# Decay attention and token/channel mixer on one core: weight casts behind the turned copies, low parts and conversions shifted, last sum with tokens on partitions

## The chip, the cores and the metric

The kernel runs on one core of a Trainium2 chip. The metric is device microseconds (us) from launch to end. The kernel before took 600.77 us (median of three runs, 600.35 to 603.7). The profiled execution is a separate one, with its own time.

TensorE is called PE here (PEld is its weight load), VectorE DVE, ScalarE ACT, GpSimd POOL, SyncE SP. SPq and ACTq are the DMA queues that SP and ACT issue into.

## The reference

The program is a chunked linear attention with a decay per head, followed by an MLP mixer. q, k, v are `[4, 8, 768, 64]` (batch, heads, tokens, head size).

```python
for b in range(nb):                      # blocks of 64 tokens
    intra = einsum('bhic,bhjc->bhij', qb, kb) * Dmask[None]
    intra = einsum('bhij,bhjd->bhid', intra, vb)
    inter = einsum('bhid,bhde->bhie', qb * lam_pow[None], kv_state)
    out[:, :, sl] = intra + inter
    kv_state = lam_block * kv_state + einsum('bhsd,bhse->bhde', kb * rev_pow, vb)
x  = out as [4, 768, 512]
u  = x + (relu(x^T @ w_tok1) @ w_tok2)^T          # w_tok1 768x256, w_tok2 256x768
y  = u + relu(u @ w_ch1) @ w_ch2                  # w_ch1 512x1536, w_ch2 1536x512
```

The mixer's weights arrive as 64-bit numbers. The kernel converts each to two 32-bit parts, a high and a low one (`w1h`, `w1l` and so on), and forms each product of the mixer as three matmuls: high by high, low by high, high by low.

## The kernel before, in words

Attention runs over 16 passes `i`, one for each pair of heads of a batch (`pairs`, four passes to a batch). It is a pipeline that is written out by hand: the order of the calls in the loop is the order of the instructions on every engine, and nothing reorders them. In pass `i` PE does `scores(i+1)` (tiles `sc`), the first half of `outputs(i)` (`xT`), the state products of pass `i+1` (`kv`), the second half of `outputs(i)`, the transposes of k and q for pass `i+2` (`kt`, and `qt` up to pass 4; from pass 5 on DVE turns q with `STREAM_TRANSPOSE`), and `turn_back(i)` (`xp`), which turns the attention output so that tokens lie on partitions. From pass 4 on, groups of matmuls of the token mixer (`ph`, `pu`) are put between these, by the table `take`.

ACT copies `xT` to `uT[b]`, copies `kt` and `qt` to `kT` and `qT`, and casts `xp` to the high part `xhi` (L354). DVE masks the scores (`a`, L299), scans the state (`sv`, L265), subtracts to get `xlo` (L355). POOL scales q (`qs`, L244), scales a part of k (`kd`, L239) and places the state (`stb`, L278, two copies). The PSUM tag `sh` has three banks, which `kv`, `kt`, `qt`, `xp`, `ph` and `pu` take in turn: a tile may start when the tile three before it has been read. So the first `xp` or `qt` behind two `kt` waits for the scan `sv` that reads `kv`. The tag `xT` has one bank.

A weight conversion (`narrow`) is eight entries of a queue `waiting`: ACT takes the magnitude (L379), DVE does five operations on 128x512 words (L380, L383, L386, L389, L392), one entry is empty, and `split` casts the high part on ACT (L374) and subtracts the low part on POOL (L375). `later(n)` takes `n` entries from that queue at fixed places in a pass. The three parts of `w_tok1` are queued in passes 0 to 2, those of `w_tok2` in passes 2 and 3 (two of them in pass 3), the four parts of the first quarter group of the channel weights in passes 6 to 9. Batches' `uT` tiles that are not yet written serve as room for raw words and results: `uT[3]` is written by attention from pass 12 on.

The channel mixer runs over six groups of hidden columns (`g`) and eight blocks of 384 tokens (`k`): `mm1` (L640), relu on ACT and low part on DVE, then `mm2` of the unit before (L661), whose result DVE adds to `uT` (L666). In all of it channels lie on partitions. In the last group the results of blocks 0 to 6 are turned by DVE and written in pieces of 32 channels; the last block is turned by PE in `finish`, copied, and written.

Of the kernel before, what the change touches and what calls it, by code (L numbers as in the profile page):

```python
# [21 lines left out]
def kernel(  # L22
# [23 lines left out]
    nc = tc.nc  # L46
# [16 lines left out]
    waiting = deque()  # L63

# [270 lines left out]
    def turn_back(i, g):  # L335
# [19 lines left out]
        nc.vector.tensor_sub(out=lo, in0=src, in1=hi.bitcast(F32))  # L355
# [7 lines left out]
    def narrow(raw, a, sg, hi, lo, view):  # L363
# [9 lines left out]
        def split():  # L373
            nc.scalar.copy(out=hi, in_=view(af))  # L374
            nc.gpsimd.tensor_sub(out=lo, in0=view(af), in1=hi.bitcast(F32))  # L375

        waiting.extend(
            [
                lambda: nc.scalar.activation(af, high.bitcast(F32), AF.Abs),  # L379
# [12 lines left out]
                lambda: nc.vector.scalar_tensor_tensor(  # L392
                    out=a, in0=a, scalar=0x7FFFFFFF, in1=sg, op0=ALU.bitwise_and, op1=ALU.bitwise_or
                ),
                lambda: None,
                split,
            ]
        )

# [84 lines left out]
    def load_group(g, pool, scratch):  # L484
# [19 lines left out]
        def convert(i):  # L504
            raw, a, sg = space[i]
            raw = raw.rearrange("p (n two) -> p n two", two=2)
            if i < 2:
                ts = slice(2 * i, 2 * i + 2)
                narrow(raw, a, sg, c1h[:, ts], c1l[:, ts], lambda x: x.rearrange("p (t f) -> p t f", t=2))
            else:  # L510
                narrow(raw, a, sg, c2h[:, i - 2], c2l[:, i - 2], lambda x: x)
# [43 lines left out]
    for i in range(-2, NI):  # L555
# [23 lines left out]
        if place:  # L579
            place()  # L580
        later(1 if work else 2)
        n = early.get(i, len(work) // 4)
        cuts = [0, n, max(n, (3 * len(work) + 1) // 4 if len(work) > 2 else len(work) // 2), len(work)]
        for n in range(3):
            for f in work[cuts[n] : cuts[n + 1]]:
                f()
                later(2 if len(work) < 3 else 1)
            if n < 2 and i >= 0:
                turn_back(i, n)
                later(1 if work else 2 + n)  # L590
            if n == 0 and i + 2 < NI:
                scale_k(i + 2)
        if 0 <= i + 3 < NI and i >= -1:
            load_v(i + 3)
# [8 lines left out]
        if 2 <= i < 4:  # L603
            convert_w2(i - 2)
        if i == 3:
            convert_w2(2)
        if i == 5:
# [5 lines left out]
        if i == 9:  # L613
            waiting.extend(split_block(0, up))
    later(99)
    att.close()
# [35 lines left out]
    def mm2(g, k, t, between=None):  # L652
# [5 lines left out]
        for jj in range(JG):  # L658
# [4 lines left out]
            if between and jj == 0:  # L663
                between()
        ub = uT[b][:, t, sh * SB : (sh + 1) * SB]
        nc.vector.tensor_add(out=ub, in0=po, in1=ub)  # L666
        if g < NG - 1 or k == len(blocks) - 1:
            return
# [12 lines left out]
    def finish(t, ylast):  # L681

        k = len(blocks) - 1
        b, sh = blocks[k]
        yp = bank("sh", f"yp{t}", SB)
        for c in range(SB // P):
            cs = slice(c * P, (c + 1) * P)
            nc.tensor.transpose(
                out=yp[:, cs], in_=uT[b][:, t, sh * SB + c * P : sh * SB + (c + 1) * P], identity=ident
            )  # L690
        es = slice(t * P, (t + 1) * P)
        src = yp.rearrange("p (c e) -> p c e", e=P)
        if t == 3:
            nc.vector.tensor_copy(out=ylast[:, :, es], in_=src)
        else:
            nc.scalar.copy(out=ylast[:, :, es], in_=src)
        to = out[b, sh * SB : (sh + 1) * SB].rearrange("(c s) e -> s c e", s=P)
        if t > 0:
            es = slice(0 if t == 1 else t * P, (t + 1) * P)
            (nc.sync if t == 2 else nc.scalar).dma_start(out=to[:, :, es], in_=ylast[:, :, es])  # L700
# [33 lines left out]
    ylast = cp.tile([P, SB // P, DM], F32, name="ylast")  # L734
    mm2(*units[-1], 0)
    mm2(*units[-1], 1)
    mm2(*units[-1], 2, between=lambda: finish(0, ylast))
    finish(1, ylast)
    mm2(*units[-1], 3, between=lambda: finish(2, ylast))
    finish(3, ylast)  # L740

# [26 lines left out]
```

## Time and profile before

| | |
|---|---|
| median of three runs | 600.77 us |
| the profiled execution, whole | 602.27 us |
| its span, first to last instruction | 600.5 us |
| PE busy | 581.5 us, 97% |
| DVE busy | 349.3 us, 58% |
| mean granted TensorE clock | 0.994 |

The span is cut by the profile into 40 slices of 15 us. PE is below nine tenths in the first five of them and in the last, and the clock row shows 9 instead of full in two of the same five. From about 72 us on PE is busy without a gap that matters until the last 5 us. The two stages that have room are the first 72 us and the tail.

### The profile page before, as it was taken

Reading aid. Unit: us, or ns where it says so; the run is one execution under the profiler, and the core shown is the slowest. Engines: PE = TensorE matmul, PEld = TensorE weight load, DVE = VectorE, ACT = ScalarE, POOL = GpSimd, SP = SyncE. Lnnn points to the kernel's source line nnn. Section 1 sums busy time; section 2 is a strip of 40 time slices with the busy share of each in tenths; the row PEclk is TensorE's granted clock in tenths of the full one; section 3 lists DMA queues with packets and bytes.
Section 4 is the critical chain, followed back from the end, with each engine's and each line's share of the span. In section 5 each row is a group of like instructions: output and inputs, shape, how many; then the busy total and the mean of one; then the engine's idle time right before and its main releaser. Section 6 shows DMA issues by size and latency. Waiting matters only on the chain.

```text
span 600.5 us, 10671 instructions
## 1 busy us (share of the span) xinstructions
PE 581.5 (97%) x4378; PEld 566.3 (94%) x4378; DVE 349.3 (58%) x663; ACT 155.4 (26%) x322; POOL 139.0 (23%) x131
## 2 busy tenths in 40 slices
PE   5979899999999999999999999999999999999997
PEld 5868799889999999999999999999999999999996
DVE  4588777886733667446534664446534664356654
ACT  3454423444223243212201221012211221011011
POOL 5646533364215358201100010001100010000000
PEclk9989899999999999999999999999999999999999
DMA  9999899999100112011200111011200200016667
GB/s 186 240 229 172 140 175 164 191 175 161 37 11 27 37 36 70 1 33 38 71 1 0 61 47 35 1 36 41 66 1 0 71 1 1 0 21 90 89 90 134
DMA packets 169648, 44.73 MB, mean 74 GB/s; under 512 B 162816, under 2 KB 163968, under 8 KB 169600
## 3 DMA queue, kind: packets, MB, share of 16 engines
q1 hardware_dynamic: 165456, 42.88, 37.6%
q10 hardware_dynamic: 4144, 1.18, 0.9%
q8 instruction: 34, 0.56, 0.4%
q14 instruction: 14, 0.11, 0.1%
HBM read 37.75 MB, written 6.29 MB: 73 GB/s over the span
## 4 chain that ended last, share of the span: by engine, by line
PE 87%; DVE 6%; DMA 4%; ACT 2%; issue 1%; SPq 0%; ACTq 0%; DVEq 0%
PE ph L640 34%; PE po L661 33%; PE ph L449 6%; PE pu L469 4%; PE xT L314 3%; PE sc L290 3%; PE xT L324 2%; DMA kn<-in_k_dram 2%; DMA uT<-in_moe_w_tok_dram 2%; PE xp L346 1%; DVE xlo L355 1%; PE kv L257 1%; DVE uT L383 1%; DVE a L299 1%; DVE uT L389 1%
## 5 line engine op out<-in xcount | busy, mean ns | idle before, releaser
L645 DVE SCALAR_TENSOR_TENSOR hl<-ph,hh 128x384 fp32r<-128x384 f32 x96 | 53.5, 558 | 164.9 <-ACT hh L644 164.9
L661 PE MATMUL po<-hh,c2h 128*128 128x384 f32 x384 | 129.4, 337 | 0.0
L640 PE MATMUL ph<-uh,c1h 128*128 128x384 f32 x384 | 129.2, 337 | 0.0
L640 PE MATMUL ph<-ul,c1h 128*128 128x384 f32 x384 | 129.2, 336 | 0.0
L640 PE MATMUL ph<-uh,c1l 128*128 128x384 f32 x384 | 129.1, 336 | 0.0
L661 PE MATMUL po<-hh,c2l 128*128 128x384 f32 x384 | 128.8, 335 | 0.0
L661 PE MATMUL po<-hl,c2h 128*128 128x384 f32 x384 | 128.6, 335 | 0.0
L644 ACT ACTIVATE hh<-ph 128x384 fp32r<-128x384 f32 x96 | 47.3, 492 | 299.5 <-PE ph L640 297.8
L666 DVE TENSOR_TENSOR uT<-po,uT 128x384 f32<-128x384 f32 x192 | 104.7, 552 | 23.5 <-PE po L661 23.4
L661 PEld LDWEIGHTS po<-hh,c2l 128*128 128x128 f32 x384 | 72.1, 188 | 0.0
L640 PEld LDWEIGHTS ph<-ul,c1h 128*128 128x128 f32 x384 | 72.1, 188 | 0.0
L661 PEld LDWEIGHTS po<-hl,c2h 128*128 128x128 f32 x384 | 72.1, 188 | 0.0
L640 PEld LDWEIGHTS ph<-uh,c1h 128*128 128x128 f32 x384 | 72.1, 188 | 0.0
L661 PEld LDWEIGHTS po<-hh,c2h 128*128 128x128 f32 x384 | 72.0, 188 | 0.0
L640 PEld LDWEIGHTS ph<-uh,c1l 128*128 128x128 f32 x384 | 72.0, 188 | 0.0
L375 POOL TENSOR_TENSOR c1l<-wa,c1h 128x512 fp32r<-128x512 f32 x10 | 12.9, 1292 | 179.9 <-ACT c1h L374 179.9
L534 POOL TENSOR_TENSOR ul<-uT,uh 128x384 fp32r<-128x384 f32 x32 | 36.0, 1157 | 37.4 <-ACT uh L533 37.4
L314 PE MATMUL xT<-a,vn 128*64 128x128 f32 x384 | 37.1, 285 | 4.3 <-ACT uT L331 4.3
L278 POOL COPY stb<-sv 64x320 f32<-64x320 f32 x32 | 26.7, 834 | 43.6 <-DVE sv L265 42.7
L299 DVE TENSOR_TENSOR a<-sc,mask 128x384 f32<-128x384 f32 x64 | 31.2, 549 | 5.8 <-PE sc L290 5.7
L324 PE MATMUL xT<-qs,stb 128*64 128x128 f32 x320 | 32.0, 278 | 0.0
L314 PEld LDWEIGHTS xT<-a,vn 128*64 128x64 f32 x384 | 22.8, 139 | 8.3 <-ACT uT L331 4.7
(80 smaller groups left out, 756.9 us busy)
## 6 DMA issues: line engine op xcount, KB each, us to landing
raw<-in_moe_w_ch_dram SPq DMA_DIRECT2D x20, 512.0 KB, 3.6
vn<-in_v_dram SPq DMA_DIRECT2D x16, 384.0 KB, 5.4
kn<-in_k_dram SPq DMA_DIRECT2D x30, 192.0 KB, 5.3
out_dram<-y SPq DMA_DIRECT2D x108, 48.0 KB, 1.9
qn<-in_q_dram SPq DMA_DIRECT2D x44, 96.0 KB, 4.1
uT<-in_moe_w_tok_dram SPq DMA_DIRECT2D x2, 1536.0 KB, 8.5
kr<-in_k_dram SPq DMA_DIRECT2D x32, 96.0 KB, 4.1
uT<-in_moe_w_ch_dram SPq DMA_DIRECT2D x4, 512.0 KB, 5.3
```

The lines of the kernel that those rows point to most:

```text
L278: nc.gpsimd.tensor_copy(out=st[r, :, h, :], in_=sv[r].rearrange("p (e c) -> p c e", c=NC - 1))
L299: nc.vector.tensor_mul(out=a, in0=sc[h].rearrange("p (c i) -> p c i", i=P), in1=mask[:, 2 * p + h, None, :].broadcast_to([P, 3, P]),)
L314: nc.tensor.matmul(out=xT[h * D : (h + 1) * D, cs], lhsT=vns[i][:, h, c, :], rhs=weights_of[i, g, h][:, cg, :], start=(cg == 0), stop=False,)
L324: nc.tensor.matmul(out=xT[h * D : (h + 1) * D, cs], lhsT=st[:, c - 1, h, :], rhs=qss[i][:, c - 1, :], start=False, stop=(cg == 2),)
L449: nc.tensor.matmul(out=ph, lhsT=w[:, c, fs], rhs=x[:, c], start=(i == 0), stop=(i == 3 * NC - 1))
L469: nc.tensor.matmul(out=pu, lhsT=h[:, kk, cs], rhs=w[:, kk, ss], start=(i == 0), stop=(i == 3 * NK - 1))
L534: nc.gpsimd.tensor_sub(out=ul[:, t], in0=ub[:, t], in1=uh[:, t].bitcast(F32))
L640: nc.tensor.matmul(out=ph, lhsT=w[:, ct, js], rhs=x[:, ct], start=(i == 0), stop=(i == 11))
L644: nc.scalar.activation(hh, ph, AF.Relu)
L645: nc.vector.scalar_tensor_tensor(out=hl, in0=ph, scalar=0.0, in1=hh.bitcast(F32), op0=ALU.max, op1=ALU.subtract)
L661: nc.tensor.matmul(out=po, lhsT=w[:, jj, cs], rhs=h, start=(i == 0), stop=(i == 3 * JG - 1))
L666: nc.vector.tensor_add(out=ub, in0=po, in1=ub)
```

## The change

Four things. (1) `split` (cast on ACT and low part on POOL) leaves the queue `waiting` and goes to a list `casts`, which is emptied at set places: behind the copies of turned k and q in each pass, in front of the next conversion's magnitude, and at the end of pass 5. A held conversion is then six entries of `waiting` instead of eight. (2) `turn_back` no longer subtracts `xlo` itself: it returns the subtraction, which runs at once in passes with token work and after the next `later` in passes without. (3) The three parts of `w_tok2` are queued in passes 2, 3, 4 instead of 2, 3, 3, and the loads and conversions of the first channel group one pass later. (4) The last block's `mm2` is done with tokens on partitions: the hidden tile is the stationary operand, 128 tokens by 512 channels are one sum (`pe`), for the last 128 tokens two sums of 256. What is added, `u`, is turned by PE beforehand, in the last group behind blocks 2, 4 and 6 (`turn_last`), copied to `ylast` by ACT, and the sum goes to memory from there without another turn.

```diff
-        nc.vector.tensor_sub(out=lo, in0=src, in1=hi.bitcast(F32))
+        return lambda: nc.vector.tensor_sub(out=lo, in0=src, in1=hi.bitcast(F32))
...
+        def magnitude():
+            flush()
+            nc.scalar.activation(af, high.bitcast(F32), AF.Abs)
+        def join():
+            nc.vector.scalar_tensor_tensor(
+                out=a, in0=a, scalar=0x7FFFFFFF, in1=sg, op0=ALU.bitwise_and, op1=ALU.bitwise_or
+            )
+            casts.append(split)
...
-                lambda: None,
-                split,
+                join,
...
         if place:
             place()
+        flush()
         later(1 if work else 2)
...
-                turn_back(i, n)
+                split_low = turn_back(i, n)
+                if work:
+                    split_low()
                 later(1 if work else 2 + n)
+                if not work:
+                    split_low()
...
-        if 2 <= i < 4:
+        if 2 <= i < 5:
             convert_w2(i - 2)
-        if i == 3:
-            convert_w2(2)
-        if 5 <= i < 9:
-            load(i - 5)
         if 6 <= i < 10:
-            convert(i - 6)
+            load(i - 6)
+        if 7 <= i < 11:
+            convert(i - 7)
...
+    def finish(c, y):
+        n = 2 if c == SB // P - 1 else 1
+        for e in range(n):
+            es = slice(e * DM // n, (e + 1) * DM // n)
+            po = bank("sc", f"pe{c}{e}", DM // n)
...
+                    nc.tensor.matmul(out=po, lhsT=h[:, cs], rhs=w[:, jj, es], start=(i == 0), stop=(i == 3 * JG - 1))
...
+            nc.vector.tensor_add(out=y[:, c, es], in0=po, in1=y[:, c, es])
+            (nc.sync if n == 2 and e == 0 else nc.scalar).dma_start(out=to, in_=y[:, c, es])
+    def turn_last(c, y):
+        yp = bank("sh", f"yp{c}", DM)
...
+        nc.scalar.copy(out=y[:, c], in_=yp)
...
+            if x == 0 and g == NG - 1 and k in (2, 4, 6):
+                turn_last(k // 2 - 1, ylast)
+    for c in range(SB // P):
+        finish(c, ylast)
```

On ACT, around pass 2, the cast of the first third of `w_tok1` moves. Before (`xT20` and `xT21` are the two halves of pass 2's output, `kt4`, `qt4` the turned k and q for pass 4):

```order
L354 CAST xhi00_332<-xp11_462 128x3x128
L374 CAST w1h_129<-uT1_61 128x512
L331 COPY uT0_60<-xT20_508 128x384
L331 COPY uT0_60<-xT21_533 128x384
L213 COPY kT4_548<-kt40_549 128x384
L213 COPY kT4_548<-kt41_554 128x384
L229 COPY qT4_547<-qt40_559 128x384
L229 COPY qT4_547<-qt41_564 128x384
L379 ACTIVATE uT1_61<-uT3_63 128x512
```

The same stretch of ACT in the changed kernel, whose lines are numbered anew (L380 is the cast, L385 the magnitude):

```order
L360 CAST xhi00_332<-xp11_462 128x3x128
L337 COPY uT0_60<-xT20_506 128x384
L337 COPY uT0_60<-xT21_531 128x384
L219 COPY kT4_546<-kt40_547 128x384
L219 COPY kT4_546<-kt41_552 128x384
L235 COPY qT4_545<-qt40_557 128x384
L235 COPY qT4_545<-qt41_562 128x384
L380 CAST w1h_129<-uT1_61 128x512
L385 ACTIVATE uT1_61<-uT3_63 128x512
```

The cast has gone from in front of six copies to behind them, and now stands just ahead of the next part's magnitude. The same holds for the second third, around pass 3; the last third's cast still stands ahead of the copy of `xT40`.

On DVE, in pass 3, from the turn of q for pass 5 to the first masked scores. Before:

```order
L218 STREAM_TRANSPOSE qT5_671<-qn5_474 128x768
L380 TENSOR_SCALAR uT1_61<-uT3_63 128x512
L383 SCALAR_TENSOR_TENSOR uT1_61<-uT3_63,uT1_61 128x512
L355 TENSOR_TENSOR xlo01_575<-xp30_689,xhi01_574 128x3x128
L386 TENSOR_SCALAR uT1_61<-uT1_61 128x512
L389 TENSOR_SCALAR uT1_61<-uT1_61 128x512
L392 SCALAR_TENSOR_TENSOR uT1_61<-uT1_61 128x512
L355 TENSOR_TENSOR xlo01_575<-xp31_701,xhi01_574 128x3x128
L380 TENSOR_SCALAR uT3_63<-uT2_62 128x512
L299 TENSOR_TENSOR a500_729<-sc500_721,mask_80 128x384
```

And in the changed kernel (L396 to L405 and L388 are the five conversion operations in their order, L361 is `xlo`):

```order
L224 STREAM_TRANSPOSE qT5_669<-qn5_472 128x768
L396 TENSOR_SCALAR uT1_61<-uT3_63 128x512
L399 SCALAR_TENSOR_TENSOR uT1_61<-uT3_63,uT1_61 128x512
L402 TENSOR_SCALAR uT1_61<-uT1_61 128x512
L405 TENSOR_SCALAR uT1_61<-uT1_61 128x512
L388 SCALAR_TENSOR_TENSOR uT1_61<-uT1_61 128x512
L361 TENSOR_TENSOR xlo01_575<-xp30_689,xhi01_574 128x3x128
L396 TENSOR_SCALAR uT3_63<-uT2_62 128x512
L399 SCALAR_TENSOR_TENSOR uT3_63<-uT2_62,uT3_63 128x512
L402 TENSOR_SCALAR uT3_63<-uT3_63 128x512
L361 TENSOR_TENSOR xlo01_575<-xp31_701,xhi01_574 128x3x128
L305 TENSOR_TENSOR a500_731<-sc500_723,mask_80 128x384
```

Two more operations of the next conversion stand ahead of the masked scores `a5` and the scan `sv5` behind them; they are missing behind `sv5`. From pass 4 to pass 6 the two orders come together again.

## Rows read from the trace of the kernel before

**Rows 1.** The page, its first part: busy us, share of the span, instructions.

```profile
PE 581.5 (97%) x4378; PEld 566.3 (94%) x4378; DVE 349.3 (58%) x663; ACT 155.4 (26%) x322; POOL 139.0 (23%) x131
```

**Rows 2.** PE's timeline: start, us, operation, count, [idle before, releaser].

```profile
32.06 0.80 PE L257 MATMUL kv<-vn,kd 128*64 128x64 f32 x20 [0.62 <-ACT kd L237]
35.08 0.69 PE L314 MATMUL xT<-a,vn 128*64 128x128 f32 x4 [2.22 <-ACT uT L331]
...
54.57 0.36 PE L449 MATMUL ph<-xhi,w1h 128*128 128x256 f32 x1
...
63.14 0.74 PE L257 MATMUL kv<-vn,kd 128*64 128x64 f32 x17 [0.48 <-POOL kd L239]
...
68.25 0.55 PE L346 MATMUL xp<-ident,uT 128*128 128x128 f32 x3 [2.20 <-DVE sv L265]
```

**Rows 3.** ACT's timeline behind the first of the two long waits.

```profile
34.03 0.62 ACT L374 CAST w1h<-uT 128x512 fp32r<-128x512 f32 x1 [1.65 <-DVE uT L392]
34.56 0.47 ACT L331 COPY uT<-xT 128x384 f32<-128x384 f32 x1
```

**Rows 4.** DVE's timeline from the landing of `w_tok1` to the scan `sv6`.

```profile
30.48 0.43 DVE L380 TENSOR_SCALAR uT<-uT 128x512 uint32<-128x512 uint32 x1 [3.62 <-DMA uT<-in_moe_w_tok_dram]
...
36.50 1.28 DVE L380 TENSOR_SCALAR uT<-uT 128x512 uint32<-128x512 uint32 x1
...
41.10 0.56 DVE L355 TENSOR_TENSOR xlo<-xp,xhi 128x384 fp32r<-128x384 f32 x1 [2.13 <-ACT xhi L354]
...
57.42 0.42 DVE L454 SCALAR_TENSOR_TENSOR hl<-ph,hh 128x256 fp32r<-128x256 f32 x1 [0.82 <-ACT hh L453]
...
59.58 0.42 DVE L454 SCALAR_TENSOR_TENSOR hl<-ph,hh 128x256 fp32r<-128x256 f32 x1 [0.68 <-ACT hh L453]
...
61.04 0.56 DVE L355 TENSOR_TENSOR xlo<-xp,xhi 128x384 fp32r<-128x384 f32 x1 [0.70 <-ACT xhi L354]
...
62.11 0.67 DVE L386 TENSOR_SCALAR uT<-uT 128x512 f32<-128x512 f32 x1
...
63.17 1.71 DVE L389 TENSOR_SCALAR uT<-uT 128x512 uint32<-128x512 uint32 x1
...
67.39 0.81 DVE L265 TENSOR_TENSOR_SCAN sv<-keep,kv 128x320 f32<-128x320 f32 x1
```

**Rows 5.** POOL's timeline beside three of those DVE operations.

```profile
35.97 1.54 POOL L244 TENSOR_TENSOR qs<-qT,lamp 128x640 f32<-128x640 f32 x1
...
61.45 1.64 POOL L239 TENSOR_SCALAR kd<-kn,mask 128x320 f32<-128x320 f32 x1
63.06 1.54 POOL L244 TENSOR_TENSOR qs<-qT,lamp 128x640 f32<-128x640 f32 x1
```

**Rows 6.** Busy time by stretch; after the engines: PEclk, DMA share, GB/s.

```profile
30.00:40.00 10.00, 7.16 (x85) 6.03 (x83) 8.38 (x14) 4.86 (x11) 5.11 (x5) 0.83 0.99 186
...
70.00:71.00 1.00, 1.00 (x6) 1.00 (x6) 0.24 (x1) 0.35 (x1) 1.00 (x1) 0.50 1.24 154
```

**Rows 7.** The chain that ended last: start, us, what.

```profile
68.80 3.66 PE ph L449 x18
...
72.78 2.15 PE ph L449 x18
...
588.40 4.71 PE po L661 x27
593.11 0.33 PE yp L688 x3
```

**Rows 8.** The tail: the last sum and the last DMA issue.

```profile
595.72 0.56 DVE L666 TENSOR_TENSOR uT<-po,uT 128x384 f32<-128x384 f32 x1 [1.16 <-PE po L661]
...
597.57 0.40 ACTq L700 DMA_DIRECT2D out_dram<-ylast  x1
```

**Rows 9.** Passes 11 and 12: a low part on DVE, the first copy into `uT[3]` on ACT.

```profile
139.18 0.42 DVE L454 SCALAR_TENSOR_TENSOR hl<-ph,hh 128x256 fp32r<-128x256 f32 x1 [1.50 <-ACT hh L453]
...
144.03 0.48 ACT L331 COPY uT<-xT 128x384 f32<-128x384 f32 x1 [2.41 <-PE xT L324]
```

More of the change, by code (lines that the diff above doesn't have):

```diff
@@ L63, with flush @@
     waiting = deque()
+    casts = deque()
+    def flush():
+        while casts:
+            casts.popleft()()
     def later(n):
@@ L361, with narrow @@
     w2l = tokp.tile([P, NK, S], F32R, name="w2l")
-    def narrow(raw, a, sg, hi, lo, view):
+    def narrow(raw, a, sg, hi, lo, view, held=True):
         low, high = raw[:, :, 0], raw[:, :, 1]
@@ L391, in narrow @@
                 ),
-                lambda: nc.vector.scalar_tensor_tensor(
-                    out=a, in0=a, scalar=0x7FFFFFFF, in1=sg, op0=ALU.bitwise_and, op1=ALU.bitwise_or
-                ),
-                lambda: None,
-                split,
-            ]
-        )
+                join,
+            ]
+        )
+        if not held:
+            waiting.extend([lambda: None, flush])
     def words(b):
@@ L650, with mm2 @@
     ys = {}
-    def mm2(g, k, t, between=None):
+    def mm2(g, k, t):
         b, sh = blocks[k]
@@ L662, in mm2 @@
                 i += 1
-            if between and jj == 0:
-                between()
         ub = uT[b][:, t, sh * SB : (sh + 1) * SB]
         nc.vector.tensor_add(out=ub, in0=po, in1=ub)
-        if g < NG - 1 or k == len(blocks) - 1:
+        if g < NG - 1:
             return
@@ L679, in mm2 @@
                     eng.dma_start(out=to[n, :, :, tt], in_=y[n * 32 : (n + 1) * 32, :, tt])
[L681 to L683 removed]
+    def finish(c, y):
+        g, k = units[-1]
         b, sh = blocks[k]
[L685 to L687 removed]
+        _, _, c2h, c2l = weights[g]
+        cs = slice(c * P, (c + 1) * P)
+        n = 2 if c == SB // P - 1 else 1
+        for e in range(n):
+            es = slice(e * DM // n, (e + 1) * DM // n)
+            po = bank("sc", f"pe{c}{e}", DM // n)
+            i = 0
+            for jj in range(JG):
+                hh, hl = hs[g, k, jj]
+                for w, h in ((c2h, hh), (c2l, hh), (c2h, hl)):
+                    nc.tensor.matmul(out=po, lhsT=h[:, cs], rhs=w[:, jj, es], start=(i == 0), stop=(i == 3 * JG - 1))
+                    i += 1
+            nc.vector.tensor_add(out=y[:, c, es], in0=po, in1=y[:, c, es])
+            to = out[b, sh * SB + c * P : sh * SB + (c + 1) * P, es]
+            (nc.sync if n == 2 and e == 0 else nc.scalar).dma_start(out=to, in_=y[:, c, es])
+    def turn_last(c, y):
+        b, sh = blocks[-1]
+        yp = bank("sh", f"yp{c}", DM)
+        for t in range(4):
             nc.tensor.transpose(
[L689 to L700 removed]
+                out=yp[:, t * P : (t + 1) * P],
+                in_=uT[b][:, t, sh * SB + c * P : sh * SB + (c + 1) * P],
+                identity=ident,
+            )
+        nc.scalar.copy(out=y[:, c], in_=yp)
     units = [(g, k) for g in range(NG) for k in range(len(blocks))]
```

22 lines of the change are left out of this document (10 added, 12 removed).

## The prediction, made before the changed kernel was run

> **What bounds the kernel now.** I read the page first: PE is busy 581.5 of 600.5 us [rows 1], so 19 us of the span are open at all, and the slices put them into the first 72 us and the tail. PE's timeline then gives the waits one by one. Between pass 2 and pass 5 they are 0.62, 2.22, 0.48 and 2.20 us [rows 2], and two shorter ones of the second's kind between. The first long one is an output copy on ACT that stands behind a cast: the cast starts at 34.03 because it waited for DVE's last conversion step, the copy comes at 34.56 [rows 3], and PE's second half of pass 2 at 35.08. The last one is another kind: the turned outputs of pass 5 need the PSUM bank that the scan `sv6` on DVE reads, and that scan starts at 67.39 [rows 2, 4]. The stretches show what such a wait costs besides: behind each of the two long ones the granted clock is 0.50 (0.83 on the mean of 30 to 40 us, 0.50 at 70) [rows 6], that is 1.2 instead of 2.4 GHz, and 18 matmuls of the token mixer take 3.66 us instead of 2.15 [rows 7].
>
> So PE waits for ACT at first sight, but I read DVE's timeline as the deeper limit. From 30.48, where the raw `w_tok1` lands, to the end of `sv6` at 67.39 + 0.81 = 68.20 DVE works through a fixed list and idles only 2.13 + 0.82 + 0.68 + 0.70 = 4.33 us [rows 4]. From about 72 us to 595 us PE waits for nothing that is worth counting, so what is won or lost before 72 us is shifted to the end as it stands.
>
> **The casts behind the copies, the low parts and the magnitudes.** In the changed kernel the copy of `xT20` no longer stands behind the cast, so the 2.22 us go from that place. What is late next is DVE: the first turned q of pass 4 needs the bank that `sv3` reads. Up to `sv3` DVE has the same seven operations in another order, all from the same landing at 30.48, and in the kernel before the operation behind `sv3` starts at 36.50 [rows 4]. So PE stands there at 36.5, as early as it can be. The gain is not the wait on ACT, it is whatever DVE idles less.
>
> DVE's list from 30.48 to `sv6` holds the same work in both kernels: three parts of `w_tok1`, two of `w_tok2`, the same scores, scans, turns and low parts. Two conversion steps stand ahead of `sv5` that stood behind it, and two parts of work behind `sv5` become shorter for it. So I count idle time only.
> - The 2.13 us at 41.10 [rows 4] came from PE being late. In the changed kernel, DVE comes from `sv3` and two conversion steps to about 38.1, and must wait there for the magnitude of the second part, which stands on ACT behind the qT copies and the cast. Those can start at 36.5: about 0.8 of PE transposes, 0.5 for the last copy [rows 3], 0.5 for the cast (34.56 less 34.03), 0.6 for the magnitude, which is the cast's own kind of operation: 38.9 to 39.0. So 0.9 is left, 1.2 gained.
> - The 0.82, 0.68 and 0.70 us [rows 4] stand where DVE waits for the first two groups of the token mixer. A group of 18 takes 2.15 us [rows 7] and a relu 0.4; DVE has three operations beside the first group (about 1.9) and two beside the second (1.0). I count 1.6 idle in place of 2.2: 0.6 gained.
> Together 1.8 us, and `sv6` ends at 66.4. PE can follow: in the kernel before, 54.57 to 68.25 is 13.7 us from the first mixer group's start, of which 0.48 and 2.20 are waits [rows 2], so 11.0 us of PE work lie between the first mixer group and that place, and the group may start as late as 55.4 (`sv5` releases its bank). Bounds: nothing, if each idle piece comes back elsewhere, and 4.3 us, the whole idle time.
>
> **The price that the order can have.** DVE's operations collide with POOL's. L380 at 36.50 took 1.28 us instead of 0.43, and ended 0.27 after POOL's `qs` (35.97 + 1.54 = 37.51); L389 at 63.17 took 1.71 and ended 0.28 after POOL's `qs` (63.06 + 1.54 = 64.60) [rows 4, 5]. L386 at 62.11, beside POOL's `kd`, took only 0.67. So one unlucky meeting costs 0.85 to 1.3 us. The changed order moves five conversion steps together and puts the low-part subtraction on POOL beside the next part's steps. The two long rows lost 0.85 and 1.28. I take the same losses after, with bounds from these rows: both gone, 2.1 us less, or three more meetings, 2.6 us more.
>
> The Trainium skill, in "SBUF — State Buffer", section "SBUF: two separate sides", has the rule behind this: the port pair that DVE and GpSimd share is an exclusive lock, whoever starts first holds it for the whole instruction, and a DVE operation in a two-port mode or with two SBUF inputs waits. By that rule nearly every conversion step that meets a POOL subtraction waits for its end. The two long rows agree with it, the 0.67 beside `kd` does not, since a full wait would have ended at 63.1 and not at 62.78.
>
> **The clock.** The half-speed stretch behind the wait at 68.25 cost 3.66 - 2.15 = 1.51 us [rows 7]. The wait that set it off shrinks to at most 1 us, since PE has 11 us of work up to there. I count 1.5 gained. The other half-speed stretch, at 35 to 38 us, also goes, but DVE's scan sets the pace there, so it is worth nothing by itself. Against it: in the changed kernel PE has several waits between 49 and 55 us (for `kd`, the copy of `xT40`, which still stands behind a cast and a magnitude, and `sv5`). A half-speed stretch may begin there. If it falls onto the first mixer group it costs up to 1.9; most of it may fall onto waiting time. I take 0.4.
>
> **The later passes.** The casts of the channel weights go one pass later. The last of them now meets `uT[3]`, which attention overwrites with a copy at 144.03. DVE's low part before it ends at 139.60 [rows 9]; two steps (0.43 each [rows 4]), a cast (0.62 [rows 3]) and POOL's subtraction (not over the 1.54 of `qs`, which has more elements [rows 5]) bring the last reader to 142.6. So it stays hidden, with 1.4 us to spare. SP's loads of these weights move with them, behind the same k, q and v loads; v for the next pass stands behind each of them and has a pass to land. PE covers all of it at 2.1 us a group. Cost: nothing; without that cover, the copy and PE behind it would be late by what exceeds the 1.4.
>
> **The tail.** Matmul work is the same: 24 of 384 columns at 4.71/27 = 0.174 us, or 12 of 512 and 12 of 256 at 0.232 and 0.119 (2.15/18) [rows 7]: 4.18 against 4.21 us. The twelve transposes stay too; three take 0.33 [rows 7], and the last three now stand in the stream, +0.33. Three copies on ACT in the last group lie beside PE. What goes is everything between the last addition and the last DMA issue: 597.57 - (595.72 + 0.56) = 1.29 us [rows 8]. The last addition has 256 instead of 384 columns: 0.42 (the 256-column `hl` [rows 4]) against 0.56, another 0.14. From that issue to the end of the span it was 600.5 - 597.57 = 2.9, with 128 rows of 3x128 numbers; now it is 128 rows of 256 on each of two queues, and I take the same. Sum: -1.29 - 0.14 + 0.33 = -1.1. Bounds: -0.3, if the writes of block 6, which SP is still issuing then, and the late writes queue up, and -1.6, if a smaller last write lands sooner.
>
> **The sum.** On the profiled execution, 602.27 = 600.5 + 1.77 around the span: -1.8 (DVE idle) - 1.5 (clock behind pass 5) + 0.4 (clock before pass 4) - 1.1 (tail) = -4.0, so 598.3. The profiled execution is 1.5 above the median of the runs, 600.77; the forecast for a median is 596.8.
>
> **The rivals.**
> - *The wait goes as a whole.* DVE meets POOL less than before, `sv5` ends at 53.2 and `sv6` at 63.4; PE then reaches the place of 68.25 at 63.9: -4.3 - 1.5 - 1.1 = -6.9, a median of 593.9. For it: the five steps stand in one row and POOL's scaled q and placed state no longer wait for a cast. Against it: the adjacent operations on POOL. 0.17.
> - *Only the tail.* The waits before `sv5` put PE at half speed for the first two mixer groups (+1.9), which eats the 1.8; pass 5 still ends with a wait of about 2 us and half speed behind it. -1.1: 599.7. For it: both long waits of before did this [rows 2, 6]. 0.20.
> - *The conversion row on DVE runs into POOL's subtractions, and `sv5` comes late.* Three more meetings at 0.85 to 1.3 in passes 3 and 4 put the first mixer group at 57.8 instead of 54.57; with half speed (+1.9) and 11.7 us (the 11.0 of work and 0.7 of a wait for `sv6`) pass 5's place is at 71.4, against 68.25 + 1.5 for the half speed that followed. +1.6 - 1.1 = +0.5: 601.3. It decides from the point where `sv5` ends after 56. This is the case that the skill's rule, taken strictly, gives. 0.13.
> The forecast has 0.50, with its own range of 595 to 598.5.
>
> **Range and chances.** 593.5 to 601.0 takes in the first three cases and most of the fourth. About 0.5% (3.0 us) is what a measurement of this kernel can tell from no change. Faster by more, below 597.8: three quarters of the forecast and the first rival, 0.55. Within: the rest of the forecast, the second rival, the small end of the third, 0.38. Slower by more, above 603.8, needs the third and a tail that gives nothing: 0.07.
>
> **What would show it.** The profile after should have no output copy behind a `w_tok1` cast in passes 2 and 3; PE waiting for `sv3` in pass 2 and for `sv5` before the first mixer group at 53 to 56 us; `sv6` ending near 66.4; granted clock 1.00 from there on; no transposes in the last 5 us, and a last DMA issue about 0.4 us behind the last matmul's end. The forecast is wrong if the conversion steps take over 1 us more than three times between 36 and 56 us, if the clock is 0.50 behind `sv6`, or if passes 6 to 12 have waits over 0.5 us.

## The result: slower by half a per cent, and the profile after

The changed kernel takes 603.24 us (median of 20 runs, 601.83 to 605.2), against 600.21 of the kernel before on the same chip (20 runs). The ratio is 1.0046, with a 95% interval of 1.0030 to 1.0062. Forecast was 596.8, so the sign is wrong and the time lies outside the range. The profiled execution took 603.91 us, with a span of 601.8; the one of before had 602.27 and 600.5.

From the first conversion step behind the landing of `w_tok1` to the end of the scan `sv6`, DVE has the same 58 instructions in both kernels (the last is only begun). That stretch, in the view of busy time by stretch (length, then PE, PEld, DVE, ACT, POOL with their counts, then PEclk, DMA share, GB/s), first of before:

```profile
30.48:68.20 37.72, 30.16 (x410) 26.96 (x406) 33.08 (x58) 19.14 (x42) 20.99 (x17) 0.95 0.96 186
```

and of the changed kernel, with its two stretches at half speed:

```profile
30.34:69.99 39.65, 31.40 (x411) 27.14 (x406) 37.95 (x58) 20.07 (x43) 20.00 (x16) 0.96 0.91 177
...
47.00:50.00 3.00, 3.00 (x26) 2.64 (x24) 2.97 (x4) 1.23 (x3) 2.86 (x4) 0.52 0.85 137
...
71.00:74.00 3.00, 3.00 (x16) 3.00 (x15) 1.37 (x3) 0.58 (x2) 2.92 (x3) 0.50 1.44 158
```

DVE's idle time fell from 37.72 - 33.08 = 4.64 to 39.65 - 37.95 = 1.70 us, by more than I had counted. But its busy time rose by 4.87 us for the same instructions. The stretch is 1.93 us longer. Where the 4.87 come from is seen in DVE's timeline after (start, us, operation; it answers to [rows 4]; the first two rows are undisturbed) beside POOL's (it answers to [rows 5]):

```profile
30.81 0.69 DVE L399 SCALAR_TENSOR_TENSOR uT<-uT,uT 128x512 uint32<-128x512 uint32 x1
31.42 0.42 DVE L402 TENSOR_SCALAR uT<-uT 128x512 f32<-128x512 f32 x1
...
39.10 1.09 DVE L402 TENSOR_SCALAR uT<-uT 128x512 f32<-128x512 f32 x1 [1.19 <-ACT uT L385]
...
41.25 1.98 DVE L388 SCALAR_TENSOR_TENSOR uT<-uT 128x512 uint32<-128x512 uint32 x1
...
48.56 1.49 DVE L402 TENSOR_SCALAR uT<-uT 128x512 f32<-128x512 f32 x1
...
52.28 1.71 DVE L399 SCALAR_TENSOR_TENSOR uT<-uT,uT 128x512 uint32<-128x512 uint32 x1
53.92 1.76 DVE L402 TENSOR_SCALAR uT<-uT 128x512 f32<-128x512 f32 x1
...
57.93 0.80 DVE L271 TENSOR_TENSOR_SCAN sv<-keep,kv 128x320 f32<-128x320 f32 x1
...
62.97 0.94 DVE L402 TENSOR_SCALAR uT<-uT 128x512 f32<-128x512 f32 x1
...
64.97 1.98 DVE L388 SCALAR_TENSOR_TENSOR uT<-uT 128x512 uint32<-128x512 uint32 x1
...
69.19 0.80 DVE L271 TENSOR_TENSOR_SCAN sv<-keep,kv 128x320 f32<-128x320 f32 x1
```

```profile
38.64 1.27 POOL L381 TENSOR_TENSOR w1l<-uT,w1h 128x512 fp32r<-128x512 f32 x1
...
41.14 1.55 POOL L250 TENSOR_TENSOR qs<-qT,lamp 128x640 f32<-128x640 f32 x1
...
48.16 1.60 POOL L381 TENSOR_TENSOR w1l<-uT,w1h 128x512 fp32r<-128x512 f32 x1
...
52.18 1.26 POOL L381 TENSOR_TENSOR w1l<-uT,w1h 128x512 fp32r<-128x512 f32 x1 [1.16 <-ACT w1h L380]
53.41 1.99 POOL L250 TENSOR_TENSOR qs<-qT,lamp 128x640 f32<-128x640 f32 x1
...
61.90 1.73 POOL L381 TENSOR_TENSOR w2l<-uT,w2h 128x512 fp32r<-128x512 f32 x1 [1.35 <-ACT w2h L380]
```

Each long DVE row ends at nearly the same distance behind the end of the POOL row that it met: `TENSOR_SCALAR` 0.28 or 0.29 us behind (40.19 behind 39.91; 50.05 behind 49.76; 55.68 behind 55.40; 63.91 behind 63.63), `SCALAR_TENSOR_TENSOR` 0.54 or 0.55 (43.23 behind 42.69). Undisturbed these take 0.42 and 0.69. Over that, the four rows beside `w1l` and `w2l` lose 0.67 + 1.07 + 1.02 + 0.52 = 3.3 us, the three beside `qs` 1.29 + 1.34 + 1.29 = 3.9. In the kernel before the two long rows lost 2.1, both to `qs`, and the subtractions of `w1l` cost DVE nothing. Rows that meet POOL's copies of the state lose about as much in both kernels (1.5 and 1.4 us). So 3.3 us from the subtractions and 3.9 - 2.1 = 1.8 from `qs` make up the 4.87, to within 0.2. One of the subtractions of before, from POOL's timeline, and the masks on DVE beside it:

```profile
33.91 1.94 DVE L299 TENSOR_TENSOR a<-sc,mask 128x384 f32<-128x384 f32 x4
...
34.73 1.27 POOL L375 TENSOR_TENSOR w1l<-uT,w1h 128x512 fp32r<-128x512 f32 x1 [6.12 <-ACT w1h L374]
```

It ran beside DVE's masking of scores, which reads PSUM and took its usual 1.94 us. This is what the change took away: before, the cast stood ahead of the output copy, so its subtraction fell onto the masks; now the cast stands behind the copies of k and q, and the subtraction falls onto the next part's steps. The Trainium skill, in "SBUF — State Buffer", section "SBUF: two separate sides", has the rule that the port pair shared by DVE and GpSimd is held by whoever started first for the whole instruction. The rows above agree with it: a DVE row that started second ends 0.14 or 0.15 us less than its undisturbed time behind POOL's end, and a POOL row that started while a DVE step was under way is longer too (1.60 and 1.73 us for the subtraction instead of 1.27, 1.99 for `qs` instead of 1.54). The rows beside POOL's `kd` (0.64 us instead of 0.42) do not.

PE's timeline after, with the waits that answer to [rows 2]:

```profile
36.47 0.88 PE L234 MATMUL qt<-ident,qn 128*128 128x128 f32 x6 [1.46 <-DVE sv L271]
...
46.34 0.87 PE L352 MATMUL xp<-ident,uT 128*128 128x128 f32 x6 [2.04 <-DVE sv L271]
...
56.20 0.55 PE L214 MATMUL kt<-ident,kn 128*128 128x128 f32 x3 [1.11 <-DVE xlo L361]
...
70.05 0.55 PE L352 MATMUL xp<-ident,uT 128*128 128x128 f32 x3 [2.04 <-DVE sv L271]
```

The wait of 2.22 us on ACT is gone, and PE stands at 36.5 for `sv3`, as forecast. The three later ones are DVE's. The chain that ended last (start, us, what) runs through the second of the two long rows of pass 4:

```profile
53.92 1.76 DVE uT L402
55.68 0.48 DVE xlo L361
56.20 0.55 PE kt L214 x3
56.75 4.45 PE ph L463 x36
...
70.05 0.55 PE xp L352 x3
70.60 3.41 PE ph L463 x18
```

Most of the 18 matmuls of the last line are at half speed again, 3.41 us against 3.66 of before [rows 7]. From the first matmul of the channel mixer to the end of the span both kernels take the same, 421.4 us (179.12 to 600.5 and 180.40 to 601.8): in these profiles the new tail is worth nothing.

### The profile page after: what moved, and what is told of

Same layout as the page of the kernel before. It is cut to its first block, busy times and chain, and to the rows that moved or that the text cites. A ratio compares the mean times of both kernels' runs of the same rounds, so it can differ in the third digit from the quotient of the medians.

```text
span 601.8 us, 10675 instructions
## 1 busy us (share of the span) xinstructions
PE 581.6 (97%) x4378; PEld 565.6 (94%) x4378; DVE 354.6 (59%) x662; ACT 155.7 (26%) x322; POOL 139.8 (23%) x131
## 4 chain that ended last, share of the span: by engine, by line
PE 88%; DVE 5%; DMA 3%; SPq 1%; POOL 1%; issue 1%; ACT 0%; ACTq 0%; DVEq 0%; POOLq 0%
PE ph L660 34%; PE po L681 33%; PE ph L463 6%; PE pu L483 5%; PE xT L320 3%; PE sc L296 3%; PE xT L330 2%; DMA qn<-in_q_dram 2%; DMA uT<-in_moe_w_tok_dram 2%; PE kv L263 1%; PE xp L352 1%; DVE a L305 1%; DVE uT L402 1%; PE pe L713 1%; DVE xlo L361 1%; DVE uT L399 1%
## 5 line engine op out<-in xcount | busy, mean ns | idle before, releaser
L681 PE MATMUL po<-hh,c2h 128*128 128x384 f32 x376 | 126.4, 336 | 0.0
L681 PE MATMUL po<-hh,c2l 128*128 128x384 f32 x376 | 126.1, 335 | 0.0
L681 PE MATMUL po<-hl,c2h 128*128 128x384 f32 x376 | 126.0, 335 | 0.0
L684 DVE TENSOR_TENSOR uT<-po,uT 128x384 f32<-128x384 f32 x188 | 102.6, 552 | 21.1 <-PE po L681 21.0
L681 PEld LDWEIGHTS po<-hh,c2l 128*128 128x128 f32 x376 | 70.6, 188 | 0.0
L681 PEld LDWEIGHTS po<-hl,c2h 128*128 128x128 f32 x376 | 70.6, 188 | 0.0
L681 PEld LDWEIGHTS po<-hh,c2h 128*128 128x128 f32 x376 | 70.5, 188 | 0.0
L337 ACT COPY uT<-xT 128x384 f32<-128x384 f32 x32 | 15.3, 479 | 56.1 <-PE xT L330 56.1
```

Source lines behind the costliest of these rows:

```text
L681: nc.tensor.matmul(out=po, lhsT=w[:, jj, cs], rhs=h, start=(i == 0), stop=(i == 3 * JG - 1))
```

## The experiments

All ratios are to the kernel before on the same chip, with 95% intervals. The texts in quotes were written before each run. The "meeting theory" in them is the reading above: a step on DVE that meets a row on POOL waits for its end.

**One part at a time.** Four kernels, each the kernel before with one of the four parts of the change alone.

*The new tail.* 

> The kernel before with the new tail alone (last sum with tokens on partitions, transposes moved into the last group). The tail theory: 1.1 to 1.3 us less than before (ratio 0.998), since the profile of the changed kernel needs 8.9 us from the last block's second layer to the end of the span, against 10.15 before, less the 1.3 us of transposes that stand earlier... of which 1.3 come back in the stream, so -1.3 from place to place and about 0 to -1.3 in all. If the tail is worth nothing because the moved transposes eat it, the ratio is 1.000.

```diff
-    mm2(*units[-1], 2, between=lambda: finish(0, ylast))
-    finish(1, ylast)
-    mm2(*units[-1], 3, between=lambda: finish(2, ylast))
-    finish(3, ylast)
+    for c in range(SB // P):
+        finish(c, ylast)
```

602.55 us, 1.0022 [1.0006, 1.0037]: no gain, rather a small loss. From the first channel matmul to the end it took 421.5 us in its profile. The reason is in the issues of the last 14 us of the changed kernel (KB each, median us to landing):

```profile
out_dram<-ylast ACTq DMA_DIRECT2D x2, 256.0 KB, 3.5
...
out_dram<-ylast SPq DMA_DIRECT2D x1, 128.0 KB, 3.6
...
out_dram<-ylast ACTq DMA_DIRECT2D x1, 128.0 KB, 3.0
```

and in the last issue of the kernel before:

```profile
out_dram<-ylast ACTq DMA_DIRECT2D x1, 192.0 KB, 2.1
```

The last issue is 1.0 us earlier counted from the first channel matmul, as forecast, but its write takes 3.0 us to land and not 2.1 as before. The four writes go out within 2.1 us. The twelve transposes (1.3 us) are also paid earlier in the stream. The small loss need not be the tail's: the granted clock of these 12 runs is 0.9925 on average, that of the 27 runs of before on this chip 0.9946, though the instructions are the same up to the tail (what that is worth is estimated at the end of the next part).

*The held casts.* 

> The casts behind the turned copies alone (with conversions of six entries instead of eight), the rest as before. Meeting theory (conversion steps on DVE run into POOL's subtractions and scalings and wait for their ends): most of the loss is here; DVE's busy time from the landing of w_tok1 to the end of the scan for pass 6 rises from 33.1 by 3 to 5 us for the same instructions, and the time by 1.5 to 3.5 us over before. Rival (the shifted conversions and low parts are to blame): this part alone gains or is equal, since the ACT wait of 2.2 us is gone.

```diff
-                lambda: None,
-                split,
+                join,
```

605.47 us, 1.0073 [1.0053, 1.0093]: alone it loses more than the whole change, and more than the 1.5 to 3.5 us expected (4.4 by the ratio). DVE's long rows are those of the changed kernel (41.64 1.98, 52.22 1.70, 53.85 1.76).

*The deferred low parts.* 

> The deferred low parts of outputs alone. Meeting theory: no POOL instruction moves, so DVE busy time in the stretch stays within 1 us of 33.1 and the time within 1 us of before. Rival (low parts come later, so the transposes of the next pass wait for their banks): 1 to 2 us slower, with waits of k's transposes for the low part on DVE.

```diff
-                turn_back(i, n)
+                split_low = turn_back(i, n)
+                if work:
+                    split_low()
                 later(1 if work else 2 + n)
+                if not work:
+                    split_low()
```

600.51 us, 0.9986 [0.9974, 0.9998]: a small gain. DVE's stretch is 36.77 us, with 32.61 busy, within the bounds expected.

*The later conversions.* 

> The later conversions alone (third part of w_tok2 and the first channel group one pass later). Both theories: within 1 us of before; DVE loses one conversion's steps from no pass before 4. A rival that blames the move of the channel weights into passes 7 to 11: 1 to 2 us slower with new waits of PE after 80 us.

```diff
-        if 2 <= i < 4:
+        if 2 <= i < 5:
             convert_w2(i - 2)
...
-        if 6 <= i < 10:
-            convert(i - 6)
+        if 7 <= i < 11:
+            convert(i - 7)
```

604.55 us, 1.0044 [1.0025, 1.0063]: not within 1 us of before, as both theories had it, but 2.6 us slower. PE's timeline has a wait there that neither full kernel has:

```profile
82.46 0.44 PE L469 MATMUL pu<-w2l,hh 128*128 128x384 f32 x1 [2.26 <-POOL w2l L375]
```

With eight entries a part that is queued one pass later is not converted in time; in the changed kernel, with six, that wait is absent. So the parts do not add up (by the ratios 4.4 us for the casts, -0.8 for the low parts, 2.6 for the conversions and 1.3 for the tail alone, 2.8 together), and this one does not explain the result.

**Is it the meeting with POOL's subtraction?** Two kernels, the changed one without the subtractions of the token weights and with each done twice.

> The changed kernel without POOL's subtraction of the low parts of the token weights (w1l and w2l are filled with zeros early on, while DVE waits for the first raw weights; their part of the products is left out in value, not in PE work). Meeting theory: the conversion steps that met w1l and w2l lose their excess (1.09, 1.49, 1.71 and 0.94 us go back to 0.42 to 0.69), DVE's busy time from the landing of w_tok1 to the end of the scan for pass 6 falls from 37.95 by 2 to 4 us for the same instructions, and the time by 1.5 to 3.5 us under the changed kernel. Rival (the order on DVE and ACT decides, not POOL): no change over 0.7 us.

```diff
             nc.scalar.copy(out=hi, in_=view(af))
+            if held:
+                return
             nc.gpsimd.tensor_sub(out=lo, in0=view(af), in1=hi.bitcast(F32))
```

598.07 us, 0.9927 [0.9904, 0.9951]. DVE's 58 instructions, by the same view of busy time:

```profile
30.77:65.40 34.63, 28.60 (x400) 24.96 (x396) 32.92 (x58) 18.85 (x42) 15.04 (x12) 1.00 0.99 199
```

These are four runs. DVE idles 1.71 us, as in the changed kernel, and is busy 5.03 us less; nothing in this stretch is at half speed. Both changes are larger than expected (2 to 4 us busy, 1.5 to 3.5 in time, against some 7). Of the 5.03, 3.3 are the four rows beside the subtractions. Most of the rest is POOL's scaled q: without a subtraction ahead of it, it still meets three steps, but costs 2.5 us (40.90 1.57, 49.93 1.30, 59.62 1.20) instead of 3.9. So where no step meets a subtraction, the changed order is worth what I had hoped. With the subtractions beside the steps, all of it is lost.

> The changed kernel with each subtraction of a low part of the token weights done twice on POOL (same result). POOL is busy 20 of 39.7 us in the stretch and would hide five more instructions of 1.3 us. Meeting theory: DVE's busy time in the stretch rises by 2 to 5 us over 37.95 and the time by 1.5 to 4 us over the changed kernel. Rival (order): within 0.7 us of it.

```diff
+            for _ in range(2 if held else 1):
                 nc.gpsimd.tensor_sub(out=lo, in0=view(af), in1=hi.bitcast(F32))
```

605.58 us, 1.0051 [1.0033, 1.0069], hardly above the changed kernel's 1.0046.

```profile
30.57:71.97 41.40, 30.63 (x402) 26.80 (x398) 39.33 (x58) 19.83 (x43) 25.17 (x20) 0.96 0.89 171
```

DVE is busy another 1.38 us and the stretch is 1.75 longer. That is below the 2 to 5 us expected, and the time is within the 0.7 us of the rival: by its own numbers the theory missed. The rows tell why. The second subtractions do make new long rows, 0.28 us behind POOL's end as above (40.45 1.38, 49.77 1.37), but they push the scaled q off two of the three steps that it met: only 66.95 1.97 is left of those. And behind pass 5 the clock stayed at 1.00 here (a slow stretch of its own lies at 54 to 58 us, inside the 41.40), while the changed kernel lost some 1.3 us there (3.41 against the 2.15 of [rows 7]):

```profile
70.00:74.00 4.00, 2.04 (x18) 1.98 (x18) 4.00 (x8) 2.65 (x6) 1.83 (x3) 1.00 1.34 154
```

The first channel matmul is only 0.45 us later (180.85 against 180.40). So in the profiles the rows follow the rule, with a smaller sum than expected, and the slow stretch that stayed away gave most of it back. The time by itself does not tell the theory from the rival.

*Control: the same edit on the kernel before.* 

> The kernel before, without POOL's subtractions of the token weights (their low parts are zeros). In the changed kernel the same edit took 1.2% (0.9927 against 1.0046 of before, about 7 us). Theory (the subtractions cost by meeting the conversion steps on DVE, and only where the order of the changed kernel puts them side by side): before runs them beside the masking of scores, which reads PSUM, so little is won here: only the rows that the pushed-back scaled q lengthens (0.85 and 1.28 us), ratio to before 0.995 to 0.999, about 1 to 3 us. Rival (the subtractions are simply work that some engine waits for, whatever the order): the same 7 us, ratio about 0.988.

604.02 us, 1.0023 [1.0011, 1.0036]: no gain at all, not even the 1 to 3 us of the theory.

```profile
31.00:68.86 37.86, 29.32 (x402) 26.12 (x398) 32.81 (x58) 19.20 (x42) 14.28 (x12) 0.95 0.95 185
```

DVE is busy as before (32.81 against 33.08). The gain expected from the two long rows did not come because the scaled q, which starts earlier here, meets two other steps (50.47 1.91, 59.31 1.59). So the rival, that the subtractions are simply work, falls: the same edit wins 1.2% in the one order and nothing in the other. It is the order that makes them dear.

**Where should the cast stand?**

> The changed kernel with the held casts put directly behind the copy of the first half of the outputs (so neither that copy nor k's and q's wait for them), and no cast in front of a magnitude. POOL's subtraction then runs while DVE masks scores, which reads PSUM. Meeting theory: no conversion step of w_tok1 meets w1l; DVE busy in the stretch 34 to 36 us; the ACT wait of 2.2 us stays away; 2.5 to 4.5 us less than the changed kernel. Rival (order of the conversion steps): at most 1 us less.

```diff
         if i >= 0:
             outputs(i, 0)
+        flush()
         place = state(i + 1) if 0 <= i + 1 < NI else None
...
         if place:
             place()
-        flush()
```

601.84 us, 1.0004 [0.9984, 1.0024]: the changed kernel with the casts behind the first output copy. By the ratios that is 2.5 us less than the changed kernel, just the least expected.

```profile
30.72:68.05 37.33, 30.17 (x409) 26.71 (x404) 33.71 (x58) 18.46 (x40) 19.88 (x16) 0.95 0.95 185
```

DVE is busy 33.71 us, 4.2 less than in the changed kernel, but idles 3.62: PE's first mixer group waits 2.04 us for `sv5`, and DVE then for the relu. One meeting is left as well, of a step of `w_tok2` with the last `w1l` (51.20 1.64).

> Early casts as in the run before this one and the deferred low parts, but the conversions' passes and the tail of the kernel before (so neither the later conversions nor the new tail). Sum of what the parts alone showed: 0.8 us from the low parts, 0 from the tail, no 2.6 from the shifted conversions; with the casts at a place without meetings 1 to 3 us more. Expected ratio to before 0.993 to 0.997; if the meetings come back in another place, 0.998 to 1.002.

602.27 us, 1.0002 [0.9989, 1.0016]: the same with before's schedule of conversions and before's tail. No better. PE waits 2.04 us for `sv5` ahead of the first mixer group, and is at half speed behind it:

```profile
57.19 0.58 PE L462 MATMUL ph<-xhi,w1h 128*128 128x256 f32 x1 [2.04 <-DVE sv L271]
```

One of the steps ahead of `sv5` meets the last `w1l` here too (52.11 1.64). That pointed at the two conversion steps that stand ahead of `sv5` because a held conversion has six entries instead of eight.

> The kernel before with the deferred low parts, and with the casts of token weights behind the first output copy; but the conversion steps on DVE stay at their old places (the queue keeps its eight entries for each part). Theory (the changed kernel loses by the places of the steps on DVE, two more ahead of the scan of pass 5, and by the meetings these bring): the wait of 2.2 us in pass 2 goes, nothing new comes, ratio to before 0.994 to 0.998. Rival (casts behind the copies lose whatever the places of the steps, because the scaled q and the subtraction on POOL change their order): ratio 1.000 to 1.007, like the two kernels with early and with held casts.

```diff
-                lambda: None,
-                split,
+                lambda: casts.append(split) if held else None,
+                lambda: None if held else split(),
```

599.31 us, 0.9958 [0.9941, 0.9975]: faster than both kernels. It differs from the last one in the two entries (and a place in pass 5 where casts are emptied), and so in where two steps stand on DVE. The stretch, and what answers to the rows above on DVE, POOL and PE:

```profile
30.56:65.92 35.36, 28.98 (x410) 25.36 (x404) 33.84 (x58) 19.04 (x41) 20.20 (x16) 1.00 1.00 199
```

```profile
42.66 1.93 DVE L305 TENSOR_TENSOR a<-sc,mask 128x384 f32<-128x384 f32 x4
...
49.72 1.31 DVE L386 TENSOR_SCALAR uT<-uT 128x512 uint32<-128x512 uint32 x1
...
53.28 0.80 DVE L271 TENSOR_TENSOR_SCAN sv<-keep,kv 128x320 f32<-128x320 f32 x1
```

```profile
42.99 1.27 POOL L381 TENSOR_TENSOR w1l<-uT,w1h 128x512 fp32r<-128x512 f32 x1 [1.28 <-ACT w1h L380]
...
50.72 1.45 POOL L381 TENSOR_TENSOR w1l<-uT,w1h 128x512 fp32r<-128x512 f32 x1
```

```profile
54.14 0.38 PE L455 MATMUL ph<-xhi,w1h 128*128 128x256 f32 x1 [1.50 <-DVE sv L271]
...
65.97 0.55 PE L352 MATMUL xp<-ident,uT 128*128 128x128 f32 x3 [0.91 <-DVE sv L271]
```

The subtractions lie beside the masks again, the output copy in pass 2 no longer stands behind a cast, and pass 5's place comes at 65.97 instead of 68.25 [rows 2]. Not all of the gain in time is DVE's: nothing is at half speed here, and how far the clock goes is estimated at the end of the next part.

> The faster variant (deferred low parts, steps on DVE at their old places, tail and schedule of before), but with the casts held back as in the changed kernel: behind the copies of turned k and q and ahead of the next magnitude. DVE has the same instructions in the same order in both; only the casts on ACT and the subtractions on POOL move. Theory (the place of the cast decides what POOL's subtraction meets: behind the first output copy it lies beside the masking of scores, behind k and q beside the next conversion steps): the meetings of the changed kernel come back, four or five more rows between 36 and 62 us over 1 us, the scan of pass 6 ends some 2 to 3.5 us later, ratio to before 0.999 to 1.004 against 0.9958. Rival (the loss was only in the two steps ahead of the scan of pass 5, which are back at their old places here): no loss, ratio 0.994 to 0.998.

```diff
             outputs(i, 0)
-        flush()
         place = state(i + 1) if 0 <= i + 1 < NI else None
...
         if place:
             place()
+        flush()
```

603.34 us, 1.0011 [0.9995, 1.0027]. DVE has the same list in the same order as in the faster variant; only the casts and subtractions have moved.

```profile
32.18:70.86 38.68, 29.96 (x392) 26.47 (x392) 35.28 (x58) 18.79 (x41) 19.78 (x16) 0.96 0.88 180
```

```profile
40.92 1.12 DVE L396 TENSOR_SCALAR uT<-uT 128x512 f32<-128x512 f32 x1 [1.16 <-ACT uT L385]
...
50.41 1.49 DVE L396 TENSOR_SCALAR uT<-uT 128x512 f32<-128x512 f32 x1
```

The stretch is 3.3 us longer, within the 2 to 3.5 expected, and the time went the theory's way. But the four or five more long rows between 36 and 62 us did not come: two came (those shown), and two of the faster variant's own went (49.72 1.31 and 57.80 1.94); a third came later, beside the scaled q (65.83 1.71). Busy time rose by only 1.44 us; 1.88 are idle time, since the magnitude on ACT stands behind the cast (1.16 instead of 0.67) and DVE, with shorter rows beside the mixer's groups, waits for ACT's relus and turned tiles again. So a late cast costs twice, on POOL and on ACT. A stretch at half speed came back as well (0.66 from 50 to 54 us). The places themselves are no measure here: `w_tok1` landed 1.6 us later than in the faster variant (32.18 against 30.56), ahead of all that was changed.

**The tail again.**

> The kernel before with the new tail, and the four last writes of block 6 issued from POOL's queue, not ACT's, so that the writes of the last block are not behind them. Theory (the new tail is no gain because its writes are issued together behind those four and take 3.0 to 3.6 us to land): the last landing falls back to 2.1 to 2.4 us, the tail is 0.7 to 1.0 shorter than with ACT's queue, ratio to before 0.9985 to 1.0005 against 1.0022 of the new tail alone. Rival (the writes land late because all the 1 MB of the tail goes out at once, whichever queue issues it): no change, 1.001 to 1.003.

```diff
-                    eng = nc.scalar if k == len(blocks) - 2 and t == 3 and n >= 2 else nc.sync
+                    eng = nc.gpsimd if k == len(blocks) - 2 and t == 3 and n >= 2 else nc.sync
```

603.7 us, 1.0029 [1.0016, 1.0042]: the theory missed.

```profile
out_dram<-y POOLq DMA_DIRECT2D x4, 48.0 KB, 3.7
out_dram<-ylast ACTq DMA_DIRECT2D x1, 128.0 KB, 4.6
out_dram<-ylast SPq DMA_DIRECT2D x1, 128.0 KB, 4.7
```

From ACT's free queue the writes land later still, 4.6 us, and POOL's take 3.7 instead of 2.1. It is not the queue that they stand in. That they go out together and share what the DMA engines move, as the rival has it, fits, but a tail with its writes spread out was not tried.

## Why the prediction was wrong, point by point

**The step that failed** is the price of the order: "I take the same losses after, with bounds from these rows: both gone, 2.1 us less, or three more meetings, 2.6 us more." The term was taken as 0 and measured 4.87, outside its own bounds. I had the rows, the rule and the sentence that the changed order "puts the low-part subtraction on POOL beside the next part's steps", and still priced it at nothing. What I had not looked up is why the subtractions cost nothing before: they lay beside the masks. Laying POOL's rows over DVE's order after the change was the way to find the seven meetings. The two kernels without the subtractions show it: -5.0 us of DVE time in the changed order (with what the scaled q then costs less), -0.3 in the old one.

**DVE's idle time** was the right term, too small: 1.8 counted, 2.9 measured. The places came out closely: PE at 36.47 (36.5 forecast), and 1.19 us of waiting for the second magnitude (0.9).

**The clock**, -1.5 + 0.4, measured nothing: two stretches at half speed before and two after. Crediting the gain was wrong in its reason too. The kernel with the new tail alone has the same instructions as before in this part, and the same wait of 2.20 us ahead of pass 5's place, but its clock differs from that of before [rows 6, 7]. By stretch:

```profile
38.00:42.00 4.00, 4.00 (x28) 3.72 (x28) 1.20 (x2) 2.98 (x7) 2.88 (x3) 0.66 0.98 133
...
70.00:74.00 4.00, 4.00 (x36) 4.00 (x35) 2.56 (x6) 2.32 (x5) 3.59 (x4) 1.00 1.16 175
```

There the first slow stretch lasted into 38 to 42 us and DVE idled 3.16 us for `xlo` instead of 2.13 [rows 4], and none followed pass 5. So "worth nothing by itself" was wrong for the first stretch, and the second is not tied to its wait. One profile cannot carry such a term. Nor does a row give the "up to 1.9" for the first mixer groups: by [rows 7] one group of 18 costs 1.51 more at half speed, and two would cost 3.0. And the slices of the profile before are read too broadly above: PE is below nine tenths in the first, third and fifth of the first five, and the clock's digit is 8 in the third and fifth and 9 in all others.

**The tail**, -1.1, measured 0: the issue came 1.0 us earlier as worked out, the landing took 0.9 longer. "I take the same" for the landing was the mis-sized part, and 0 lies outside its bounds. That bound of -0.3 allowed for writes that queue up; why they land late is not shown, only that ACT's queue is not the reason.

**`sv5` and the first mixer group.** I wrote that the group waits for `sv5`. It started at 56.50, before `sv5` (57.93); PE had been released by the low part `xlo`, which is in the chain from 55.68 to 56.16, behind the two long rows. So here the group cannot stand in the bank that `sv5` reads, and the three banks are not taken strictly in turn, as the kernel's description has it. In the changed kernel without subtractions the group waits 0.24 us for ACT's copy of turned k. In the faster variant and in four others (the casts alone, the subtractions done twice, the two with early casts) it does wait for `sv5`. Why the bank differs the traces do not show, and part of what tells these kernels from the changed one may lie there.

**What held.** No output copy stands behind a `w_tok1` cast in passes 2 and 3, passes 6 to 12 have no wait over 0.4 us, the later channel conversions stayed hidden. And the third rival, "The conversion row on DVE runs into POOL's subtractions, and `sv5` comes late", is what happened: decided by `sv5` ending behind 56 (58.73), the first group at 56.50 (57.8 forecast), pass 5's place at 70.05 (71.4 forecast), a median of 603.24 (601.3 forecast, with a gain in the tail that did not come). Its half speed for the first mixer groups did not come: the 36 matmuls took 4.45 us. It had 0.13, and the range, which I said took in most of it, ended at 601.0, below its 601.3. My own test for it, more than three steps over 1 us between 36 and 56, counts seven in the profile after, but it was badly set: by the same count the kernel before has four, two of them beside POOL's copies of the state at 1.14 us.

**What stays open** is where all of the 3.0 us lies. The profiled executions differ by 1.6 us only, 0.3 of it outside the span. The clock does not seem to be it: the 20 runs of the changed kernel had a granted clock of 0.9949 on average, and the 27 runs of before on each of two other chips 0.9946 and 0.9942 (for the chip of the result the clocks of before are not on record). Over such 27 runs the span is longer by some 0.46 us for each 0.001 of mean clock less, by a straight line through them. By this estimate 1.0 of the 1.3 us that the new tail lost alone is clock, and 1.2 of the 1.4 that the control without subtractions lost. It is also 2.0 of the 4.4 us that the changed kernel without subtractions won over before, and 1.8 of the 2.5 of the faster variant (0.9982 over its runs, against 0.9942). Whether their shorter waits brought the higher clock is not shown. Of the 3.2 us by which the faster variant and the one with the casts held back differ, 0.9 is clock by the same estimate, so some 2.3 is left for the place of the cast.

## What to carry to other kernels

Before moving a cast or any producer, lay the instructions that it feeds on the other engines over what the neighbours do at the new time. The GpSimd subtraction cost nothing here where it ran beside VectorE's masks, which read PSUM; beside steps from SBUF to SBUF it cost 0.5 to 1.1 us each, four times. Where a queue's length sets the places of later steps, keep empty entries when you take one out: that was worth 0.44% (1.0002 against 0.9958), the clock included.

## What the runs showed of the hardware that was not expected

- A conversion step on DVE that starts while POOL's subtraction, scaled q or state copy runs ends some 0.28 us (`TENSOR_SCALAR`) or 0.54 us (`SCALAR_TENSOR_TENSOR`) behind the end of that POOL row; beside POOL's `kd` it loses only 0.2, and the masks from PSUM lose nothing (1.93 to 1.95 us for four in every kernel).
- In the three profiles whose instructions agree up to the tail (before, and the two with the new tail alone), the first step behind `w_tok1`'s landing starts at 30.48, 30.78 and 31.11 us, and the slow stretches lie at different places.
- Writes of 48 KB issued from POOL took 3.7 us to land, against 2.1 from ACT.
